# Retention and ELU feed-forward on one core: w_out in 4 KB pieces, features in even and odd tiles, and small moves between engines

## The chip, the cores and the metric

The kernel runs on one core of one Trainium2 chip. Such a core has TensorE (PE) for matmuls, with weight loads shown apart (PEld), VectorE (DVE), ScalarE (ACT) and GpSimd (POOL) for element-wise work, SyncE (SP), which here only issues DMAs, and 16 DMA engines between the chip's memory and SBUF. Matmul results go to PSUM, in banks. The metric is the device time of one execution in microseconds; a time of a kernel is the median of its runs.

## The reference, cut to what matters

```python
# q, k, v: (8, 8, 576, 64), batch x heads x positions x head dim; moe_w_in: (512, 2048); moe_w_out: (2048, 512)
def _attn_ref(q, k, v):
    scores = 1.0 / np.sqrt(64) * np.matmul(q, k.transpose(0, 1, 3, 2))
    gamma = 1.0 - 2.0 ** (-5.0 - np.arange(8))
    rel = pos[:, None] - pos[None, :]
    Dmat = np.where(rel >= 0, gamma[:, None, None] ** rel[None, :, :], 0.0)
    return np.matmul(scores * Dmat[None], v)

def _moe_ref(x, w_in, w_out):              # x: 4608 tokens x 512
    h = x @ w_in
    g = np.where(h > 0.0, h, np.exp(np.minimum(h, 0.0)) - 1.0)
    return g @ w_out
```

The retention result of the eight heads is put side by side into rows of 512, one row for each of 8 x 576 tokens, and goes through the feed-forward layer. All inputs and the output are float32. The hidden features, 2048 of them, are summed over in the second product, so their order does not matter as long as the columns of w_in, g and the rows of w_out agree.

## The kernel before, in words

**Retention.** The decay is split into a factor on q and one on k, so a unit of work is: load q, k and v for one stretch of positions and heads (`load`), multiply q and k by their factors and round to bf16 (`cast`, `cast_qk`, `cast_v`), turn them so that head dimensions lie on partitions (`turn`, a DMA transpose, or `turn_pe`, TensorE transposes into PSUM with a copy back), multiply k by q (`scores`), mask the product within a chunk of 64 (`masks`, on VectorE, tile `pt`), and add what earlier chunks contribute through a running state (`state`, `prefix`, `inter`). The state of a chunk lies in the same PSUM bank (x0 or x1, pool `ps_x`) as the unit's output; VectorE reads it into the tiles `mid` and `end`, and small copies bring them in bf16 into `s_pair` (`put_mid`, `put_end`) or, at the end of a batch, into `s_last` (`put_last`), which the last 64 positions of each batch need much later. `put_x` writes a unit's output, turned, into `xt`. Units are numbered from 0; the first twelve are coarse (256 positions, four heads), so that "the sixth unit" is `load(5)`, `cast(5, ...)` and `turn_pe(5, ...)`. A call `stretch(u)` makes the scores, masks and states of unit u and finishes unit u - 1.

**Feed-forward.** FFN1 (`ffn1`, `ffn1_half`) makes one tile of 128 hidden features for 512 tokens, or two tiles for 256 tokens, with four matmuls per tile over the 512 inputs; the weights that are loaded are 128 columns of `w_in_sb` (tile `ph`). `elu` does the activation with two passes on ScalarE (L607, L610) and one on VectorE (L611), which writes `g`. FFN2 (`ffn2`) multiplies g by `w_out_sb`, 512 wide, over 16 feature tiles into one bank per 128 tokens (tile `pm`), which ScalarE copies out (`ot`).

**Weights.** `weights(k)` lists, for one staging tile of 512 KB, the two DMA sources and the places in SBUF: k = 0 to 7 are w_in, k = 8 to 15 are w_out, with two blocks of 128 features each (L163). `load_w` issues two DMAs of 256 KB on SyncE, each partition receiving 2 KB from one row; `cast_w` rounds each half to bf16, mostly on GpSimd. Staging tiles and q/k tiles share ten buffers.

**The order.** All instructions are pinned in program order on each engine (`pin`), so a wait on one engine holds up all that stands behind it there. Up to the first twelve units the order is written by hand. The first four units come first; then FFN1 of the first 512 tokens, one tile at a time (`one(ft, ...)`), with FFN2 rows behind it: `row(i)` is the two matmuls that add feature tile i to two blocks of output. L834 and L835 say which rows stand behind which tile: 

```python
    behind = {4: (0, 1), 11: ()}
    behind.update({ft: (ft - (3 if ft < 11 else 4),) for ft in range(5, 16) if ft != 11})
```

These tiles' banks come from two pools: even tiles take x0 and x1 in turn, odd tiles the three banks of `ps_h`, of which one holds the second output block. Then the fifth to eighth units are woven with `quad(i)`, four FFN2 matmuls of the other two output blocks, and with halves of FFN1 of the next batch (`some`). From the ninth unit on, lists of FFN1 and FFN2 jobs are mixed by `stage`, and a unit's step is put between them at due times. SyncE issues its loads in the order in which the program names them (L810 to L816, L878, L879, L884), DMA transposes among them.

Of the kernel before, what the change touches and what calls it, by code (L numbers as in the profile page):

```python
# [17 lines left out]
def kernel(  # L18
# [9 lines left out]
    nc = tc.nc  # L28
# [5 lines left out]
    P = 128  # L34
# [4 lines left out]
    KJ = DM // P  # L39
# [23 lines left out]
    pin = tc.keep_in_program_order  # L63
    def mm(*a, **kw):
        pin(nc.tensor.matmul(*a, **kw))  # L65
# [77 lines left out]
    w_in_sb = const.tile([P, KJ, DF], BF16, name="w_in_sb")  # L143
    w_out_sb = const.tile([P, NFT, DM], BF16, name="w_out_sb")
# [3 lines left out]
    tt = {"v": nc.vector.tensor_tensor, "p": nc.gpsimd.tensor_tensor}  # L148
    staged = {}

    def weights(k):
        for h in range(2 * (k < 2)):

            r, c = slice(2 * h * P, 2 * (h + 1) * P), slice(k * 2 * P, (k + 1) * 2 * P)
            yield h, moe_w_in[r, c].rearrange("(j p) c -> p j c", j=2), w_in_sb[:, 2 * h : 2 * h + 2, c]
        for i in (2 * k, 2 * k + 1) if k > 1 else ():
            n, j = divmod(i, KJ)
            if n < KJ:
                c = slice(n * 512, (n + 1) * 512)
                yield i % 2, moe_w_in[j * P : (j + 1) * P, c], w_in_sb[:, j, c]  # L160
            else:
                f = i - KJ * KJ
                yield i % 2, moe_w_out[f * P : (f + 1) * P, :], w_out_sb[:, f, :]  # L163

    def load_w(k):
        staged[k] = raw.tile([P, 2, 4, 2, D], FP32, name="rqk", tag="rqk").rearrange("p i h e d -> p i (h e d)")
        for h, src, dst in weights(k):
            pin(nc.sync.dma_start(staged[k][:, h] if k > 1 else staged[k][:, h].rearrange("p (j c) -> p j c", j=2), src))  # L168

# [11 lines left out]
    def fine(u):  # L181
        return seq[u][0] >= 3
# [7 lines left out]
    def load(u, what="qkv"):  # L190
        b, T, w = seq[u]
        if u not in rawt:
            rawt[u] = (raw.tile([P, 2, 4, 2, D], FP32, name="rqk", tag="rqk"),
                       raw.tile([P, 4, 2, D], FP32, name="rv", tag="rv", bufs=5))
        rqk, rv = rawt[u]
        parts = [{"q": (rqk[:, 0], q), "k": (rqk[:, 1], k), "v": (rv, v)}[x] for x in what]
        if fine(u):
            t = u % 4
            for dst, src in parts:
                pin(nc.sync.dma_start(  # L200
                    dst.rearrange("p a e d -> p (a e) d"), src[b, :, t * P : (t + 1) * P, :].rearrange("h p d -> p h d"),
                ))
            return
        for dst, src in parts:
            pin(nc.sync.dma_start(  # L205
                dst.rearrange("p h e d -> p h (e d)"),
                src[b, 4 * w : 4 * w + 4, 2 * P * T : 2 * P * (T + 1), :].rearrange("h (p e) d -> p h (e d)", e=2),
            ))

    def cast_qk(u, i, eng, es=(0, 1)):  # L210
        b, T, w = seq[u]
        if fine(u):
            pin(tt[eng](  # L213
                natt[u][0][:, i].rearrange("p e h d -> p (e h) d"), rawt[u][0][:, i].rearrange("p a e d -> p (a e) d"),
                (gqf, gkf)[i][:, u % 4].unsqueeze(2).to_broadcast([P, H, D]), ALU.mult,
            ))
            return
        x = rawt[u][0][:, i].rearrange("p h e d -> p e h d")
        g = (gq, gk)[i][:, 2 * T : 2 * T + 2, 4 * w : 4 * w + 4].unsqueeze(3).to_broadcast([P, 2, 4, D])
        for e in es:  # L220
            pin(tt[eng](natt[u][0][:, i, e], x[:, e], g[:, e], ALU.mult))  # L221

    def cast_v(u, eng):
        pin(engines[eng](natt[u][1], rawt[u][1]))  # L224

    def cast(u, q="p", k="p", v="p"):
        if u >= NS:
            return
        qkn = nat.tile([P, 2, 2, 4, D], BF16, name="qkn", tag="qkn")
        vn = nat.tile([P, 4, 2, D], BF16, name="vn", tag="vn", bufs=5)  # L230
        natt[u] = qkn, vn
        if q:
            cast_qk(u, 0, q)
        if k:
            cast_qk(u, 1, k)
        if v:
            cast_v(u, v)

    def flat(u):
        return natt[u][0].rearrange("p i e h d -> p (i e h d)")  # L240

    def turn(u):
        if u < NS:
            trt[u] = tpool.tile([P, 8, P], BF16, name="qkT", tag="qkT")
            pin(nc.sync.dma_start_transpose(trt[u], flat(u)))
# [19 lines left out]
    def new_x():  # L265
        for c in range(2):
            xps[c] = ps_x.tile([P, 512], FP32, name="x", tag=f"x{c}")
        begun.clear()
# [105 lines left out]
    def drop(u):  # L374
        natt.pop(u)
        ptt.pop(u)
        trt.pop(u)
        score_ps.pop(u, None)
# [75 lines left out]
    def blocks(dst, src, eng):  # L454
        for i in range(2):
            pin(engines[eng](dst[half(i), :, half(i)], src[half(i)]))  # L456

    def put_last(b, w, src, eng):
        for i in range(2):
            pin(engines[eng](s_last[b % 3][half(w), :, i], src[half(i)]))  # L460
# [4 lines left out]
    def put_end(u, eng="p"):  # L465
        b, T, w = seq[u]
        if T:
            put_last(b, w, total[w], eng)
        else:
            blocks(s_first[w], total[w], eng)  # L470
# [68 lines left out]
    def stretch(u, put="p", end="p"):  # L539
        old = u - 1 in natt and u - 1 in ptt  # L540
        rider = late.pop() if late else None
        new_x()
        if rider is not None:
            inter_rider(rider)
        if old:
            inter(u - 1)
        if u < NS:
            scores(u)
            if fine(u):
                state(u)  # L550
            masks(u)
        if u in rides:
            scores_rider(rides[u])
        if old:
            values(u - 1)
        if rider is not None:
            values_rider(rider)
        if u < NS and not fine(u):
            state(u)
        if old:  # L560
            put_x(u - 1)
            drop(u - 1)
        if rider is not None:
            put_rider(rider)
        if u < NS:
            if fine(u):
                prefix_fine(u)
            else:
                prefix_mid(u, put)
                prefix_end(u, end)  # L570
        if u in rides:
            masks_rider(rides[u])
            late.append(rides[u])
# [16 lines left out]
    def xt_tile(g):  # L590
        if g == B:
            return xtail
        if g not in xts:
            xts[g] = xpool.tile([P, 2, KJ, 2 * P], BF16, name="xt", tag="xt")
        return xts[g]
# [22 lines left out]
    def ffn1(g, ft, pool=None, tag="ph", **kw):  # L618

        ph = (pool or ps_h).tile([P, TG], FP32, name="ph", tag=tag)  # L620
        for j in range(KJ):
            mm(ph, w_in_sb[:, j, ft * P : (ft + 1) * P], xt_tile(g)[:, :, j], start=(j == 0), stop=(j == KJ - 1))
        gtile(g, ft // 2, 0)
        elu(gts[g, ft // 2][:, :, ft % 2], ph, pairs, **kw)

    def ffn1_half(g, p, hf, **kw):

        ph = ps_h.tile([P, TG], FP32, name="ph", tag="ph")
        for f in range(2):
            for j in range(KJ):  # L630
                mm(ph[:, f * 2 * P : (f + 1) * 2 * P], w_in_sb[:, j, (2 * p + f) * P : (2 * p + f + 1) * P],
                   xt_tile(g)[:, hf, j], start=(j == 0), stop=(j == KJ - 1))
        elu(gtile(g, p, hf).rearrange("p f n -> p (f n)"), ph, **kw)

# [121 lines left out]
    first = [ps_x.tile([P, TG], FP32, name="ph", tag=f"x{ft}") for ft in range(2)]  # L756

    def part(ft, *js):
        for j in js:
            mm(first[ft], w_in_sb[:, j, ft * P : (ft + 1) * P], xt_tile(0)[:, :, j], start=(j == 0), stop=(j == KJ - 1))  # L760

    masks(3, (1,))
    cast_w(0, " v")
# [46 lines left out]
    for kk in (4, 5, 10, 11, 6, 7, 12, 13):  # L810
        load_w(kk)
    load(4)
    for kk in (14, 15):
        load_w(kk)
    for u in range(5, 10):
        load(u)  # L816
    F = {0: {}, 1: dict(pool=ps_h, tag="ph"), 2: dict(pool=ps_h, tag="ph"), 3: {}}

    def row(ft):
# [11 lines left out]
    for kk in (8, 9, 4, 5, 10, 11):  # L831
        cast_w(kk)

    behind = {4: (0, 1), 11: ()}  # L834
    behind.update({ft: (ft - (3 if ft < 11 else 4),) for ft in range(5, 16) if ft != 11})  # L835
    for ft in range(4, 8):
        one(ft, behind[ft])
    for kk in (6, 7, 12, 13):
# [3 lines left out]
    cast(4, "p", "p", None)  # L842
    cast_w(14)
    cast_w(15)
    put_end(2)
    put_end(3)
    half1 = f1h(1, 0)

    def some():
# [7 lines left out]
    quad(0)  # L857
    turn_pe(4, "vs", pool=ps_x, tags=("x0", "x1"))
    cast_v(4, "s")
    cast(5, "v", "p", None)  # L860
    quad(1)
    quad(2)
    stretch(4, "p")
# [5 lines left out]
    cast_v(5, "s")  # L869
    cast(6, "v", "p", None)  # L870
    quad(3)
    stretch(5, end=None)
    quad(4)
    turn_pe(6, "vs")
    cast_v(6, "s")
    cast(7, "v", "p", None)
    put_end(5)
    turn(7)  # L878
    load(10)  # L879
    quad(5)  # L880
    stretch(6, "p")
# [76 lines left out]
    c = [j for g, hf in twos[E:] for j in f2(g, (2 * hf, 2 * hf + 1))]  # L958
    at = {id(x): i // 8 for i, x in enumerate(a)}
    jobs = weave(a, c)  # L960
    n = 0
    phases = [[] for _ in range(len(ones) - E + 1)]
    for x in jobs:
        n = at.get(id(x), n)
# [50 lines left out]
```

## Time and profile before

| What | us |
|---|---|
| Median of 3 runs | 303.43 (303.04 to 304.12) |
| The profiled execution | 303.18 |
| its span, first to last instruction | 301.4 |
| TensorE busy | 289.8 (96%) |
| ScalarE busy | 210.8 (70%) |
| GpSimd busy | 175.4 (58%) |
| VectorE busy | 175.1 (58%) |
| DMA, mean over the span | 180 GB/s |

In rows of the profile a line such as `L611 DVE SCALAR_TENSOR_TENSOR g<-e,ph` is line, engine, operation, and output from inputs by the program's names. In a timeline a row has start, duration, engine, line, what, how many instructions, and in brackets the idle time of the engine before it with what ended it; a row with x4 stands for four neighbouring instructions. In the chain of work a row has start, duration and what the chain went through. [...] Some matmul records are missing, so a row may say x3 for four matmuls. SPq rows are the issuing of DMAs on SyncE.

### The profile page before, as it was taken

To read this page: it belongs to the slowest core of one execution; us is meant where nothing else is said; L and a number is where in the kernel's file an instruction comes from. 1 tells how busy PE (TensorE), PEld (TensorE's weight loads), DVE (VectorE), ACT (ScalarE), POOL (GpSimd) and SP (SyncE) were. 2 spreads that over 40 slices of the span, in tenths; PEclk is the share of its full clock that TensorE was granted. 3 is DMA by queue.
4 is the path that set the end of the run, shared out by engine and by line. 5 is a ranking of instruction groups with operands and counts; after the bars stand their busy time and mean duration, and the time that the engine had idled before them with its cause. 6 is when DMAs were issued, how large, how long until landed. Compare 5 with 4: busy or idle time off the path is not lost.

```text
span 301.4 us, 9038 instructions
## 1 busy us (share of the span) xinstructions
PE 289.8 (96%) x3587; PEld 176.0 (58%) x3624; DVE 175.1 (58%) x355; ACT 210.8 (70%) x430; POOL 175.4 (58%) x344
## 2 busy tenths in 40 slices
PE   8789999999999999999999999999999999999995
PEld 5444446776676666667767675544444444456654
DVE  4846557765556756666776766768675734332210
ACT  4669847967766777767777887777777776764531
POOL 5689887687957585858496887468852300011000
PEclk9999999999999999999999999999999999999999
DMA  7999999989999999999999999999860100001012
GB/s 208 307 360 353 353 306 285 220 244 165 248 191 214 176 221 211 199 201 207 202 188 213 195 202 211 190 237 177 173 90 37 38 35 36 37 35 70 37 70 70
DMA packets 133418, 54.33 MB, mean 180 GB/s; under 512 B 107712, under 2 KB 127424, under 8 KB 133376
## 3 DMA queue, kind: packets, MB, share of 16 engines
q1 hardware_dynamic: 130624, 45.04, 77.3%
q0 software_dynamic: 2672, 8.65, 8.5%
q8 instruction: 28, 0.46, 0.7%
q14 instruction: 14, 0.11, 0.1%
q10 hardware_dynamic: 80, 0.07, 0.1%
HBM read 36.70 MB, written 9.44 MB: 153 GB/s over the span
## 4 chain that ended last, share of the span: by engine, by line
PE 80%; DMA 10%; SPq 3%; issue 2%; ACT 2%; DVE 1%; POOL 0%; DVEq 0%
PE pm L65 36%; PE ph L65 36%; DMA rqk<-in_moe_w_out_dram 5%; PE x L65 4%; SPq L205 3%; PE sc L65 3%; DMA rqk<-in_q_dram 2%; DMA rqk<-in_moe_w_in_dram 2%; PE pe L65 1%; ACT ph L610 1%; DVE pt L318 1%; ACT e L607 1%; SPq L168 1%; PE ptr L256 0%; DVE qkn L221 0%
## 5 line engine op out<-in xcount | busy, mean ns | idle before, releaser
L611 DVE SCALAR_TENSOR_TENSOR g<-e,ph 128x512 bf16<-128x512 f32 x128 | 86.4, 686 | 84.6 <-ACT ph L610 81.1
L65 PE MATMUL ph<-xt,w_in_sb 128*128 128x256 bf16 (+1 forms) x768 | 128.7, 308 | 0.2 <-DVE g L611 0.2
L65 PE MATMUL pm<-w_out_sb,g 128*128 128x512 bf16 x478 | 123.8, 379 | 3.1 <-issue 2.1
L607 ACT ACTIVATE e<-ph 128x512 f32<-128x512 f32 x144 | 86.0, 597 | 52.5 <-PE ph L65 51.8
L65 PEld LDWEIGHTS <-w_in_sb 128*128 128x128 bf16 x896 | 86.4, 98 | 50.3 <-issue 0.6
L610 ACT ACTIVATE ph<-ph 128x512 f32<-128x512 f32 x144 | 83.9, 591 | 0.0
L65 PEld LDWEIGHTS <-g 128*128 128x128 bf16 x512 | 48.7, 98 | 43.8
L664 POOL DMA_DIRECT2D out_dram<-ot x35 | 19.9, 569 | 44.6 <-ACT ot L654 44.2
L436 POOL CAST s_fine<-run 64x256 bf16<-64x256 f32 x40 | 15.8, 396 | 42.2 <-DVE run L405 33.2
L654 ACT COPY ot<-pm 128x512 f32<-128x512 f32 x35 | 20.4, 587 | 15.1 <-PE pm L65 15.0
L611 DVE SCALAR_TENSOR_TENSOR gt<-e,ph 128x512 bf16<-128x512 f32 x16 | 10.9, 687 | 18.8 <-ACT ph L610 17.2
L213 POOL TENSOR_TENSOR qkn<-rqk,gqf 128x512 bf16<-128x512 f32 x20 | 21.1, 1053 | 0.4
L213 POOL TENSOR_TENSOR qkn<-rqk,gkf 128x512 bf16<-128x512 f32 x20 | 20.9, 1046 | 0.0
L221 POOL TENSOR_TENSOR qkn<-rqk,gk 128x256 bf16<-128x256 f32 x23 | 14.2, 638 | 4.4 <-DMA rqk<-in_k_dram 4.2
L65 PE MATMUL ph<-xtail,w_in_sb 128*128 128x256 bf16 x128 | 16.5, 273 | 0.0
L368 ACT CAST xt<-x 128x256 bf16<-128x256 f32 x40 | 12.9, 378 | 4.8 <-PE x L65 4.8
L405 DVE TENSOR_TENSOR run<-sc,run 128x256 f32<-128x256 f32 x35 | 14.9, 424 | 1.2
L224 POOL CAST vn<-rv 128x512 bf16<-128x512 f32 x24 | 14.6, 608 | 1.4
L318 DVE TENSOR_TENSOR pt<-sc,mask 128x1024 bf16<-128x1024 f32 x11 | 13.4, 1218 | 0.5 <-PE sc L65 0.4
L311 DVE TENSOR_TENSOR pt<-sc,mask_t 128x512 bf16<-128x512 f32 x20 | 13.7, 684 | 0.0
L456 POOL CAST s_pair<-mid 64x128 bf16<-64x128 f32 x24 | 6.9, 288 | 10.7 <-DVE mid L405 6.4
L442 POOL CAST s_fine<-run 64x256 bf16<-64x256 f32 x30 | 11.8, 395 | 1.8
(94 smaller groups left out, 261.4 us busy)
## 6 DMA issues: line engine op xcount, KB each, us to landing
rqk<-in_q_dram SPq DMA_DIRECT2D x32, 256.0 KB, 4.4
rqk<-in_k_dram SPq DMA_DIRECT2D x32, 256.0 KB, 5.2
rv<-in_v_dram SPq DMA_DIRECT2D x32, 256.0 KB, 5.6
out_dram<-ot POOLq DMA_DIRECT2D x31, 256.0 KB, 3.5
rqk<-in_moe_w_in_dram SPq DMA_DIRECT2D x16, 256.0 KB, 5.9
rqk<-in_moe_w_out_dram SPq DMA_DIRECT2D x16, 256.0 KB, 5.4
rqt<-in_q_dram SPq DMA_DIRECT2D x8, 128.0 KB, 5.5
rqt<-in_k_dram SPq DMA_DIRECT2D x8, 128.0 KB, 4.9
```

Of the source, the lines that this page charges most:

```text
L65: pin(nc.tensor.matmul(*a, **kw))
L213: pin(tt[eng](natt[u][0][:, i].rearrange("p e h d -> p (e h) d"), rawt[u][0][:, i].rearrange("p a e d -> p (a e) d"), (gqf, gkf)[i][:, u % ...
L221: pin(tt[eng](natt[u][0][:, i, e], x[:, e], g[:, e], ALU.mult))
L224: pin(engines[eng](natt[u][1], rawt[u][1]))
L318: pin(nc.vector.tensor_tensor(ptt[u].rearrange("p i h n -> p (i h) n"), sc.rearrange("p i (h n) -> p (i h) n", h=2), m.to_broadcast([P, 4, ...
L405: pin(nc.vector.tensor_tensor(dst, a, b, ALU.add))
L436: pin(nc.gpsimd.tensor_copy(s_fine[u % 2][half(1), :, i], new[half(i), 0]))
L607: pin(nc.scalar.activation(e, ph, AF.Exp))
L610: pin(nc.scalar.activation(ph, ph, AF.Relu))
L611: pin(nc.vector.scalar_tensor_tensor(dst, view(e), -1.0, view(ph), ALU.add, ALU.min))
L654: pin(nc.scalar.copy(ot, pm))
L664: pin((queue or nc.gpsimd).dma_start(dst, src))
```

## The change

- A new function `features(ft)` names the 128 features of a tile: of each 256 neighbouring features the even ones for an even tile, the odd ones for an odd tile. FFN1 takes its weights from these columns of `w_in_sb`, that is with a step of two (`ffn1`, `ffn1_half`, `part`).
- w_out follows: a partition now holds two neighbouring rows. For k = 9 to 15 both come in one DMA of 512 KB, 4 KB for each partition; k = 8 is still loaded by two DMAs, of every second row.
- FFN2 rows of the first 512 tokens stand four tiles behind FFN1 throughout; before, it was three for tiles 5 to 10, with two rows behind tile 4 and none behind tile 11.
- The last states of the third and fourth unit are copied by ScalarE instead of GpSimd and stand later in the program, behind `cast_v(4, "s")`.
- q of the sixth unit is scaled by GpSimd instead of VectorE.
- The tenth unit's loads stand behind the eighth unit's turn on SyncE instead of ahead of it.
- `stretch(5, "p", ...)` and `put_end(5, "p")` name the value that was the default.

```diff
+    def features(ft):
+        return slice(ft // 2 * 2 * P + ft % 2, (ft // 2 + 1) * 2 * P, 2)
+
     def weights(k):
...
                 f = i - KJ * KJ
-                yield i % 2, moe_w_out[f * P : (f + 1) * P, :], w_out_sb[:, f, :]
+                yield i % 2, moe_w_out[features(f), :], w_out_sb[:, f, :]
...
     def load_w(k):
         staged[k] = raw.tile([P, 2, 4, 2, D], FP32, name="rqk", tag="rqk").rearrange("p i h e d -> p i (h e d)")
+        if k > KJ * KJ // 2:
+            n = k - KJ * KJ // 2
+            pin(nc.sync.dma_start(
+                staged[k].rearrange("p e c -> p (e c)"),
+                moe_w_out[2 * n * P : 2 * (n + 1) * P, :].rearrange("(p e) c -> p (e c)", e=2),
+            ))
+            return
...
-            mm(ph, w_in_sb[:, j, ft * P : (ft + 1) * P], xt_tile(g)[:, :, j], start=(j == 0), stop=(j == KJ - 1))
+            mm(ph, w_in_sb[:, j, features(ft)], xt_tile(g)[:, :, j], start=(j == 0), stop=(j == KJ - 1))
...
-                mm(ph[:, f * 2 * P : (f + 1) * 2 * P], w_in_sb[:, j, (2 * p + f) * P : (2 * p + f + 1) * P],
+                mm(ph[:, f * 2 * P : (f + 1) * 2 * P], w_in_sb[:, j, features(2 * p + f)],
...
-            mm(first[ft], w_in_sb[:, j, ft * P : (ft + 1) * P], xt_tile(0)[:, :, j], start=(j == 0), stop=(j == KJ - 1))
+            mm(first[ft], w_in_sb[:, j, features(ft)], xt_tile(0)[:, :, j], start=(j == 0), stop=(j == KJ - 1))
...
-    for kk in (14, 15):
-        load_w(kk)
-    for u in range(5, 10):
-        load(u)
+    load_w(14)
+    load_w(15)
+    load(5)
+    load(6)
+    load(7)
+    load(8)
...
-    behind = {4: (0, 1), 11: ()}
-    behind.update({ft: (ft - (3 if ft < 11 else 4),) for ft in range(5, 16) if ft != 11})
+    behind = {ft: (ft - 4,) for ft in range(4, 16)}
...
     cast_w(14)
     cast_w(15)
-    put_end(2)
-    put_end(3)
     half1 = f1h(1, 0)
...
     cast_v(4, "s")
-    cast(5, "v", "p", None)
+    put_end(2, "s")
+    put_end(3, "s")
+    cast(5, "p", "p", None)
...
-    stretch(5, end=None)
+    stretch(5, "p", end=None)
...
-    put_end(5)
+    put_end(5, "p")
     turn(7)
+    load(9)
     load(10)
```

## The prediction

> **What bounds the kernel now.** I read the page first, then the busy time by stretch, the list of TensorE's waits, the chain of work over the early part, and last the engines' timelines around the waits found. The page:
>
> ```profile
> span 301.4 us, 9038 instructions
> ...
> PE 289.8 (96%) x3587; PEld 176.0 (58%) x3624; DVE 175.1 (58%) x355; ACT 210.8 (70%) x430; POOL 175.4 (58%) x344
> ```
>
> TensorE is busy for 96% of the span. The busy time by stretch (stretch, its length, then each engine) tells where the rest lies:
>
> ```profile
> 18.70:37.90 19.20, 19.08 (x102) 8.67 (x97) 10.11 (x16) 16.54 (x33) 17.66 (x30) 1.00 1.04 351
> 37.90:50.70 12.80, 11.80 (x193) 6.98 (x195) 9.47 (x18) 7.53 (x17) 10.18 (x23) 1.00 1.14 299
> 50.70:62.00 11.30, 10.84 (x149) 8.79 (x149) 7.00 (x13) 10.50 (x23) 8.10 (x19) 1.00 1.18 252
> ```
>
> and so do the waits of TensorE from 18.5 us to the end:
>
> ```profile
> PE ptr L256 <- DVE end L405: 0.6, 1, 0.6
> ...
> PE ph L65 <- DVE g L611: 0.2, 1, 0.2
> ```
>
> So there is little to win: 1.0 us of idle time from 37.9 to 50.7, 0.5 us up to 62. The early waits are single ones, and after 62 us TensorE has none on another engine, so what is saved or lost before is carried to the end. The first 18.7 us do not contain what the diff moves. The chain shows where the 0.6 us comes from:
>
> ```profile
> 29.17 5.51 DMA rqk<-in_moe_w_out_dram
> ...
> 34.74 7.05 DMA rqk<-in_q_dram
> 41.80 0.02 issue
> 41.82 0.30 DVE qkn L221
> ```
>
> It is the DMA stream, weights and then the sixth unit's q, landed at 41.79. VectorE scales that q first and only then masks the fifth unit and reads its states, which sit in the bank into which the sixth unit is turned.
>
> **The change part by part.**
>
> *FFN2 rows one tile later (L834, L835).* TensorE, then VectorE, around 24 us, and from the whole chain the pace of eight 256-wide and four 512-wide matmuls:
>
> ```profile
> 23.50 1.03 PE L65 MATMUL pm<-w_out_sb,g 128*128 128x512 bf16 x3
> 24.54 1.02 PE L65 MATMUL ph<-xt,w_in_sb 128*128 128x512 bf16 x4
> ```
> ```profile
> 23.80 0.69 DVE L611 SCALAR_TENSOR_TENSOR g<-e,ph 128x512 bf16<-128x512 f32 x1 [0.31 <-ACT ph L610]
> ```
> ```profile
> 82.75 0.87 PE ph L65 x8
> ...
> 261.44 0.86 PE pm L65 x4
> ```
>
> A 512-wide matmul takes 0.216 us, a 256-wide one 0.109. Rows 0 and 1 (four matmuls, one not recorded) fill 23.50 to 24.36; tile 5 starts at 24.54, 0.05 us after the g that ends at 24.49. That is tile 2's, whose bank tile 5 takes: a hidden wait of 0.18 us. With row 1 moved behind tile 5, TensorE arrives at 23.93 and still waits until 24.54. The displaced row (2 x 0.216 us) is paid at tile 11, which had no row behind it. Cost +0.43 us on the path; it takes away no wait that the list shows.
>
> *The sixth unit's q on GpSimd, last states on ScalarE (L845, L846, L860).* TensorE, VectorE, ScalarE and GpSimd around 42 us:
>
> ```profile
> 39.22 0.61 PE L256 MATMUL ptr<-ident,qkn 128*128 128x128 bf16 x8
> 39.66 1.89 PE L65 MATMUL pm<-w_out_sb,g 128*128 128x512 bf16 x8
> 41.48 0.42 PE L65 MATMUL sc<-qkT 64*64 64x128 bf16 x16
> 41.73 0.29 PE L65 MATMUL x<-vn,qkn 64*64 64x64 bf16 x16
> 41.96 1.90 PE L65 MATMUL pm<-w_out_sb,g 128*128 128x512 bf16 x7
> 44.49 0.61 PE L256 MATMUL ptr<-ident,qkn 128*128 128x128 bf16 x8 [0.63 <-DVE end L405]
> ```
> ```profile
> 41.82 0.85 DVE L221 TENSOR_TENSOR qkn<-rqk,gq 128x256 bf16<-128x256 f32 x2 [1.56 <-DMA rqk<-in_q_dram]
> 42.60 1.21 DVE L318 TENSOR_TENSOR pt<-sc,mask 128x1024 bf16<-128x1024 f32 x1
> 43.73 0.28 DVE L416 COPY mid<-x 128x128 f32<-128x128 f32 x1
> 44.14 0.29 DVE L405 TENSOR_TENSOR end<-x,mid 128x128 f32<-128x128 f32 x1
> ```
> ```profile
> 43.68 1.07 ACT L654 COPY ot<-pm 128x512 f32<-128x512 f32 x2 [2.71 <-PE pm L65]
> 45.13 0.58 ACT L257 COPY qkT<-ptr 128x512 bf16<-128x512 bf16 x1 [0.38 <-PE ptr L256]
> ```
> ```profile
> 40.23 1.34 POOL L173 CAST w_out_sb<-rqk 128x512 bf16<-128x512 f32 x2 [0.89 <-DMA rqk<-in_moe_w_out_dram]
> 41.51 1.66 POOL L460 CAST s_last<-end 64x128 bf16<-64x128 f32 x4
> 43.24 1.18 POOL L221 TENSOR_TENSOR qkn<-rqk,gk 128x256 bf16<-128x256 f32 x2
> ```
>
> Before, the eight matmuls from 41.96 end at 43.69 and the transposes start at 44.49: a wait of 0.80 us. After, TensorE is 0.43 later: scores from 41.91 to 42.33. VectorE, free of q, starts pt when they end, about 42.38; mid comes 1.13 later (43.73 - 42.60), end 0.41 after mid (44.14 - 43.73) and lasts 0.29: done at 44.21, transposes at 44.27 (0.06 later, as now). TensorE arrives at 44.12, so a wait of 0.15 remains: -0.65 us.
>
> What covers the moves: GpSimd gives up 1.66 us of states and takes q for 1.18 us, the price of its k. The four small copies on ScalarE have no row there; GpSimd's 1.66 us for them is the nearest, zero and twice that the ends. ScalarE idles for 2.71 us before its ot copies, so even 2.7 us would be covered and I take 0; without that cover the ot copies would start up to 0.6 us later. Late next is ScalarE's copy of the turned k. It stands behind the ot copies, which move 0.43 later (44.11 to 45.18), and would end at 45.7, about when TensorE wants the scores of the sixth unit: +0.03.
>
> *w_out in 4 KB pieces (L163, L167, L168).* SyncE's issues: weights in 2 KB pieces, then units in 512 B pieces, then the eighth unit's turn:
>
> ```profile
> 21.96 2.27 SPq L168 DMA_DIRECT2D rqk<-in_moe_w_out_dram  x4
> 24.55 2.27 SPq L168 DMA_DIRECT2D rqk<-in_moe_w_in_dram  x4
> ...
> 41.77 0.78 SPq L205 DMA_DIRECT2D rqk<-in_q_dram  x1
> ...
> 44.40 0.73 SPq L205 DMA_DIRECT2D rqk<-in_q_dram  x1
> ...
> 50.43 1.97 SPq L245 DMA_TRANSPOSE qkT<-qkn  x1
> ```
>
> Four weight transfers of 256 KB pass in 2.6 us (0.65 each), three unit transfers in 2.63 (0.88 each). At 8 and 32 pieces on each of 16 engines that is 81 and 27 ns a piece, of which some 9 ns do not grow with its size. 512 KB in 4 KB pieces would save 8 x 9 ns, 0.07 us; the seven of them 0.5 us, with zero as one end and 7 x 8 x 27 ns = 1.5 us as the other. The path gains none of it: TensorE waits for no weights, and the q that was waited for now stands on GpSimd behind the last w_out. Against it, 512 KB land as one, so the first of two casts starts up to 0.65 us later. For the last piece: landed about 40.9 (41.57 less one cast of 0.67), less 0.5; two casts of 1.34 end at 41.7, q at 42.9, k at 44.1. The k half is turned from 44.49 on (four of eight transposes behind 44.27), so this is covered: 0. If the stream gains nothing, k ends at 44.6: +0.1.
>
> *The eighth unit's turn ahead of the tenth unit's loads (L816, L878).* SyncE had issued those loads by 50.43, so the issue gains next to nothing, and the transfer at most the three loads ahead of it, 3 x 0.88 = 2.6 us. No wait of TensorE is on a turned unit, so 0. The loads, and the ninth unit's turn behind them, go back by as much; two units' work lies between them and their use, so 0 again, and at most 2.6 if nothing lay between.
>
> *Tiles of even and odd features (L622, L631, L760).* No instruction is added, but the 896 weight loads of FFN1 read every second column:
>
> ```profile
> L65 PE MATMUL ph<-xt,w_in_sb 128*128 128x256 bf16 x512 | 65.4, 273 | 0.2 <-DVE g L611 0.2
> ...
> L65 PE MATMUL ph<-xtail,w_in_sb 128*128 128x256 bf16 x128 | 16.5, 273 | 0.0
> ```
> ```profile
> L65 PEld LDWEIGHTS <-w_in_sb 128*128 128x128 bf16 x896 | 86.4, 98 | 50.3 <-issue 0.6 <-DVE xt L372 0.2
> ```
>
> No row has a strided load. Eight pairs of a load and a 128-wide matmul took 0.44 us (39.22 to 39.66), so a contiguous load repeats within 55 ns. If the stride halves its speed it needs 110 ns, at the edge of the 109 ns of the 256-wide matmul that covers it. Lower end 0 (a gain has no room: the matmuls set the pace), upper end the 98 ns doubled with nothing overlapped, 640 x 87 ns = 56 us. I take 0, by the pairs, which are nearest.
>
> [...]
>
> **Sum.** +0.43 - 0.65 + 0.03 = -0.2 us. The profiled execution took 303.18 (span 301.4, 1.8 around it), so 303.0 on its scale. The median of the runs shown, 303.43, is 0.25 above it, so 303.2 as a median.
>
> **Rivals.**
> - *Strided loads are paid (slower).* For it: nothing shows them free, and half speed is already at the edge. [...] It decides from 109 ns a load: at 112, 640 x 3 ns = 1.9 us, 305.1; at the far end 359. [...]
> - *The row's move is free (faster).* If tile 5 does not hang on tile 2's bank, -0.65 + 0.03 stands alone: 302.8. Against it: the 0.05 us between that g and tile 5.
> - *GpSimd becomes the bound.* It is busy 17.66 of 19.20 us up to 37.9. If the whole landings put its casts back by 0.4 us more than reckoned, the transposes wait for k instead of VectorE; at a further 0.65 us the second term of the sum is gone, 303.9.
> - *The move of q does nothing,* if in other executions q lands early enough and the 0.80 us are not there: +0.43 alone, 303.9.
>
> **How the numbers follow.** Forecast 0.5, strided loads 0.2 (0.17 near 305, 0.03 far out), the other three 0.1 each. Runs of this kernel can tell about 0.3%, 0.9 us, from no change. Strided loads lie beyond it; of the others, with a spread of runs from 303.04 to 304.12, some tenth falls out on either side: faster 0.12, same 0.61, slower 0.27. Range 302.5 (row free, a low run) to 305.0 (loads at 112 ns); the likeliest's own is 302.7 to 303.9.
>
> **What would show it.** Right: tile 5 still at 24.5 with 0.6 us idle ahead of it; pt of the fifth unit right behind its scores; a wait of 0.2 us or less before the sixth unit's transposes; eight 256-wide matmuls still in 0.87 us. Wrong: eights above 0.87, a wait for GpSimd before transposes or rows, tile 5 before 24.5.

## The result, and the profile after

The changed kernel takes 304.70 us in the median of 21 runs (303.14 to 306.86), the kernel before 303.37 beside it (302.23 to 304.63, 21 runs): a ratio of 1.0047, 95% interval 1.0030 to 1.0065. Forecast were 303.2 and a change of -0.2; it is slower by 1.3 us. Below, turns and loads are named as in the code: `turn(8)` is the ninth unit's turn, `load(9)` the tenth unit's loads.

The profiled execution took 305.54 (span 303.8). From the page, and TensorE's waits from 18.5 us on (who waited for whom: total, times, longest):

```profile
span 303.8 us, 9068 instructions
...
PE 293.6 (97%) x3624; PEld 175.6 (58%) x3624; DVE 175.5 (58%) x353; ACT 212.1 (70%) x434; POOL 174.7 (58%) x342
```
```profile
PE sc L65 <- DMA qkT<-qkn: 1.4, 2, 1.0
...
PE ph L65 <- DVE g L622: 0.4, 1, 0.4
```

TensorE's 3.8 us more of busy time than before are mostly a matter of records: of the same 3624 matmuls, 37 were not recorded before. The busy time by stretch, as before but 0.81 us later, since this execution starts its FFN1 by that much later:

```profile
19.51:38.71 19.20, 18.75 (x102) 8.50 (x95) 10.64 (x17) 16.21 (x33) 16.55 (x30) 1.00 1.02 360
38.71:51.51 12.80, 12.80 (x199) 7.31 (x198) 8.94 (x17) 9.05 (x21) 10.40 (x21) 1.00 1.00 263
51.51:62.81 11.30, 10.89 (x150) 8.78 (x148) 6.83 (x13) 10.49 (x23) 8.12 (x19) 1.00 0.94 234
62.81:80.00 17.19, 15.83 (x225) 10.75 (x223) 10.46 (x17) 10.67 (x22) 12.75 (x27) 1.00 1.26 226
```

The 1.0 us of idle time in the second stretch is gone (0.3 of it were gaps in which a matmul was not recorded, which leaves 0.6 to 0.8 of waiting), the first lacks some 0.3 more, and after 62.8, where TensorE had no wait on another engine, 1.4 us are idle. The wait of the sixth unit's transposes for VectorE is gone from the list, the wait of tile 5 for g is longer, and a new one is the largest: scores wait for a DMA transpose. TensorE's timeline, before and after:

```profile
18.72 0.60 PE L65 MATMUL ph<-xt,w_in_sb 128*128 128x512 bf16 x2
...
64.65 0.42 PE L65 MATMUL sc<-qkT 64*64 64x128 bf16 x16
...
69.68 0.42 PE L65 MATMUL sc<-qkT 64*64 64x128 bf16 x16
```
```profile
19.53 0.61 PE L65 MATMUL ph<-xt,w_in_sb 128*128 128x512 bf16 x2
...
25.35 1.02 PE L65 MATMUL ph<-xt,w_in_sb 128*128 128x512 bf16 x4 [0.45 <-DVE g L622]
...
43.20 1.90 PE L65 MATMUL pm<-w_out_sb,g 128*128 128x512 bf16 x8
45.09 0.61 PE L267 MATMUL ptr<-ident,qkn 128*128 128x128 bf16 x8
...
66.49 0.42 PE L65 MATMUL sc<-qkT 64*64 64x128 bf16 x16 [1.03 <-DMA qkT<-qkn]
...
71.92 0.42 PE L65 MATMUL sc<-qkT 64*64 64x128 bf16 x16 [0.33 <-DMA qkT<-qkn]
```

TensorE's rows overlap (the eight transposes from 45.09 last 0.61 us, and the next matmuls start 0.44 after them, at 45.53), so gaps given "by the starts" leave the overlap out.

FFN1 of the first tokens starts 0.81 us later (19.53 against 18.72). In the traces of this document it starts between 18.67 and 19.98 us, with and without the parts of the change. Here the delay is already there when SyncE issues the first weights (10.62 us against 9.79), ahead of anything the diff moves. Counted from that start, the first half tile of the next batch begins 0.1 us earlier than before (51.39 - 19.53 against 50.66 - 18.72), and the scores that use `turn(8)` begin 1.0 us later (46.96 against 45.93); those that use `turn(9)` 1.4 later (52.39 against 50.96). 0.8 of start, -0.1, and 1.5 of turns with what follows them (an idle stretch of 1.20 by the starts, and the 0.33 of the last row) make up most of the 2.4 us between the spans.

SyncE's issues, after and (one row) before, then GpSimd's row for k of `turn(7)`, after, and the busy time from 50 to 52 us, before and after (last two columns: mean share of the 16 DMA engines, GB/s):

```profile
46.51 0.82 SPq L216 DMA_DIRECT2D rv<-in_v_dram  x1
50.80 1.34 SPq L256 DMA_TRANSPOSE qkT<-qkn  x1
52.19 0.57 SPq L216 DMA_DIRECT2D rqk<-in_q_dram  x1
...
55.50 0.38 SPq L216 DMA_DIRECT2D rv<-in_v_dram  x1
56.00 4.29 SPq L256 DMA_TRANSPOSE qkT<-qkn  x1
...
63.50 5.14 SPq L256 DMA_TRANSPOSE qkT<-qkn  x2
```
```profile
54.86 1.25 SPq L245 DMA_TRANSPOSE qkT<-qkn  x1
```
```profile
49.28 1.50 POOL L232 TENSOR_TENSOR qkn<-rqk,gk 128x256 bf16<-128x256 f32 x2
```
```profile
50.00:52.00 2.00, 1.99 (x16) 1.50 (x16) 1.36 (x3) 1.39 (x4) 1.50 (x6) 1.00 1.10 287
```
```profile
50.00:52.00 2.00, 2.00 (x58) 1.43 (x51) 1.90 (x4) 1.28 (x4) 1.53 (x5) 1.00 0.15 36
```

`turn(7)` cannot be issued before GpSimd has scaled its k (49.28 + 1.50 = 50.78; issued 50.80). In the kernel before, three loads of `load(9)` were under way then. Now they stand behind the waiting turn, SyncE issues nothing from 47.33 to 50.80, and the queue runs empty: 36 GB/s instead of 287. Then `load(9)`, `load(10)`, `turn(8)` and three output stores of GpSimd want to pass together; the issue of `turn(8)` alone took 4.29 us (1.25 before). The chain of work of the changed kernel goes through `turn(9)`:

```profile
63.41 0.09 POOL vn L235
63.50 8.38 DMA qkT<-qkn
71.88 0.04 issue
```

Counted from the start of FFN1, `turn(9)` is issued when it was before (63.50 - 19.53 and 62.69 - 18.72 are both 43.97), but lands 3.7 us later. By this chain, taking away the wait for `turn(8)` alone would not help: TensorE would wait longer for `turn(9)`.

### The profile page after: what moved, and what is told of

Read it like the earlier page. It is cut to its first block, busy times and chain, and to the rows that moved or that the text cites. A ratio compares the mean times of both kernels' runs of the same rounds, so it can differ in the third digit from the quotient of the medians.

```text
span 303.8 us, 9068 instructions
## 1 busy us (share of the span) xinstructions
PE 293.6 (97%) x3624; PEld 175.6 (58%) x3624; DVE 175.5 (58%) x353; ACT 212.1 (70%) x434; POOL 174.7 (58%) x342
## 4 chain that ended last, share of the span: by engine, by line
PE 85%; DMA 4%; ACT 3%; SPq 3%; POOL 2%; issue 1%; DVE 1%; POOLq 0%
PE pm L65 39%; PE ph L65 37%; PE x L65 4%; PE sc L65 3%; DMA qkT<-qkn 3%; SPq L216 3%; DMA rqk<-in_k_dram 2%; ACT ph L621 1%; PE pe L65 1%; ACT e L618 1%; POOL qkn L232 1%; POOL s_pair L467 1%; PE ptr L267 0%; DVE pt L329 0%; DVE g L622 0%
## 5 line engine op out<-in xcount | busy, mean ns | idle before, releaser
L65 PE MATMUL pm<-w_out_sb,g 128*128 128x512 bf16 x512 | 129.8, 379 | 0.0
L447 POOL CAST s_fine<-run 64x256 bf16<-64x256 f32 x40 | 16.0, 400 | 41.9 <-DVE run L416 34.0
L65 PE MATMUL sc<-qkT 64*64 64x64 bf16 (+1 forms) x512 | 11.6, 204 | 1.6 <-DMA qkT<-qkn 1.4
```

The costliest lines, as they stand in the source:

```text
L447: pin(nc.gpsimd.tensor_copy(s_fine[u % 2][half(1), :, i], new[half(i), 0]))
```

## The experiments

Each kernel ran beside the kernel before on the same chip; a ratio is to that, with a 95% interval. The chip of the result is not recorded and is called the first here; e1 to e4 ran on a second (which may be the same), e5, e6, e7 and e11 on a third, e12, e15 and the second runs of e2 and of the changed kernel on a fourth, e16, the third run of the changed kernel and the second ones of e1 and e11 on a fifth. From e7 on the expectations count loads as the code does ("the ninth unit's loads" are `load(9)`), turns as above.

**e1: the loads back.**

```diff
     load(8)
+    load(9)
...
     turn(7)
-    load(9)
     load(10)
```

> The changed kernel with the tenth unit's loads ahead of the eighth unit's turn again; all else of the change stays. Theory (the moved loads make the turns of the ninth and tenth unit late): TensorE's waits on turned units, 1.4 us in the changed kernel, vanish; time 1.5 us below the changed kernel, near 303.2, 0.2 below the kernel before. Rival (the 4 KB pieces or the other moves disturb the DMA stream, and the turns are late for that): the waits stay at 1 us or more and the time stays near 304.7. In both, tile 5 still waits 0.6 us and the sixth unit's transposes 0.15.

Measured: 303.43 (303.10 to 303.88), ratio 0.9981 (0.9961 to 1.0001). No wait for a turned unit. The timeline and the stretch from 50 to 52 us:

```profile
64.78 0.42 PE L65 MATMUL sc<-qkT 64*64 64x128 bf16 x16
...
69.82 0.42 PE L65 MATMUL sc<-qkT 64*64 64x128 bf16 x16
```
```profile
50.00:52.00 2.00, 1.86 (x15) 1.41 (x17) 1.40 (x3) 1.37 (x4) 1.43 (x6) 1.00 1.11 286
```

All the rest of the change is in this kernel; only the position of three loads differs. Counted from the start of FFN1 the two scores begin 0.1 us sooner than before, but to the end of the span both take 282.7 us: one trace shows no gain from the rest of the change.

**e2: that part alone.** The kernel before, with `load(9)` behind `turn(7)`.

```diff
-    for u in range(5, 10):
+    for u in range(5, 9):
...
     turn(7)
+    load(9)
     load(10)
```

> The kernel before with one edit: the tenth unit's loads behind the eighth unit's turn. Theory (late turns): TensorE waits for the turned ninth and tenth units, 1 to 2 us together, none elsewhere that is new; time 1 to 2 us above the kernel before, 304.4 to 305.4. Rival (disturbance by the 4 KB pieces): no such wait, time within 0.3 of the kernel before.

Measured: 304.75 (303.31 to 306.02), ratio 1.0034 (1.0014 to 1.0054). So the part alone costs about 1 us in the median. Its trace (an execution of 304.19) doesn't show the wait: `turn(8)` landed at 64.69, 1.0 us ahead of the scores at 65.68, where the kernel before has 3.2. What this trace has over that of the kernel before, 1.0 us, lies ahead of the moved loads in the main: FFN1 starts 0.38 later, and the sixth unit's transposes wait 0.5 longer. Once more, on the fourth chip:

> The kernel before with only the ninth unit's loads behind the eighth unit's turn, once more, for a second trace: the first took 304.2 us and showed no wait on a turned unit, but only 1.0 us between the landing of the ninth unit's turn and its use, where before has 3.2. Theory: what is lost in the median of 1.1 us is lost in such executions in which that 1.0 us is used up, so either the wait shows now, or the slack is again below 1.5 us and the time near before.

Measured: 303.88 (302.64 to 306.14), 1.0012 (0.9988 to 1.0036); the trace is that of an execution of 303.17, and `turn(8)` landed at 64.23, 0.4 us ahead of its use. The second interval includes a ratio of 1, and the wait was never seen in this kernel; that it makes the executions above 304.5 is inferred from the spent slack.

**e3 and e4: the other moves alone.** e3 is the kernel before with q of the sixth unit on GpSimd and the last states on ScalarE; e4 the kernel before with rows four tiles behind.

```diff
-    put_end(2)
-    put_end(3)
...
-    cast(5, "v", "p", None)
+    put_end(2, "s")
+    put_end(3, "s")
+    cast(5, "p", "p", None)
```
```diff
-    behind = {4: (0, 1), 11: ()}
-    behind.update({ft: (ft - (3 if ft < 11 else 4),) for ft in range(5, 16) if ft != 11})
+    behind = {ft: (ft - 4,) for ft in range(4, 16)}
```

> The kernel before with q of the sixth unit on GpSimd and the last states on ScalarE, nothing else. By the sum of the prediction: the wait of 0.80 us before the sixth unit's transposes falls to about 0.15, time 0.65 us below the kernel before (302.8). Rival (q lands early enough in other executions): no wait there to remove, time the same.

> The kernel before with the FFN2 rows four tiles behind throughout, nothing else. By the sum of the prediction: tile 5 starts 0.6 instead of 0.18 us after TensorE is free, 0.43 us more up to there. Whether it reaches the end: VectorE's mask of the fifth unit waits for q, not for TensorE, so a part is hidden in the 0.80 us wait before the sixth unit's transposes, which then shrinks by up to 0.43; time 0 to 0.43 us above the kernel before. Rival (the row is free): tile 5 starts earlier than 0.6 us after, and nothing changes.

Measured: e3 303.76, ratio 1.0002 (0.9983 to 1.0020); e4 303.93, 1.0002 (0.9984 to 1.0021). TensorE's timeline of e3, then its waits in e4:

```profile
30.20 0.59 PE L65 MATMUL pm<-w_out_sb,g 128*128 128x512 bf16 x2 [0.78 <-POOL w_out_sb L173]
...
44.16 1.90 PE L65 MATMUL pm<-w_out_sb,g 128*128 128x512 bf16 x7
46.06 0.73 PE L256 MATMUL ptr<-ident,qkn 128*128 128x128 bf16 x8
```
```profile
PE ph L65 <- DVE g L611: 0.7, 1, 0.7
PE ptr L256 <- DVE end L405: 0.4, 1, 0.4
```

In e3 the transposes follow with a gap of 0.16 by the starts, as reckoned, but this execution started late (FFN1 at 19.98), and rows three tiles behind then wait 0.78 for w_out. In e4 tile 5 waits 0.6 to 0.7, as reckoned, and the transposes' wait is 0.52 by the starts instead of 0.80: part of the 0.43 comes back there. Neither effect is large enough for the medians.

**e5 and e6: the even and odd tiles, without and with the 4 KB pieces.** The kernel before with `features` in FFN1 and in the rows of w_out; e6 also with the DMA of 512 KB.

```diff
-                yield i % 2, moe_w_out[f * P : (f + 1) * P, :], w_out_sb[:, f, :]
+                yield i % 2, moe_w_out[features(f), :], w_out_sb[:, f, :]
...
-            mm(ph, w_in_sb[:, j, ft * P : (ft + 1) * P], xt_tile(g)[:, :, j], start=(j == 0), stop=(j == KJ - 1))
+            mm(ph, w_in_sb[:, j, features(ft)], xt_tile(g)[:, :, j], start=(j == 0), stop=(j == KJ - 1))
```

> The kernel before with nothing but the tiles of even and odd features: the 896 weight loads of FFN1 read every second column, w_out is still loaded in 2 KB pieces (its rows chosen to match), and the order of the work is untouched. If strided loads cost nothing, as the pace of the changed kernel says: a weight load of 98 ns in the mean, eight 256-wide matmuls still in 0.87 us, time within 0.3% of before. If they are paid and something else in the changed kernel hid it: loads above 109 ns and 1.9 us or more on top of before.

> The kernel before with the tiles of even and odd features and w_out in 4 KB pieces, rows, engines and the order of the loads as before. Prediction's cost of the pieces: 0, the stream at most 0.5 us shorter and hidden. But rows stay three tiles behind, and 512 KB land as one, so the first row of a pair can come later: if rows wait for it, a wait of TensorE for the cast w_out of up to 0.7 us shows in the early part and the time rises by as much; if not, time within 0.3% of before.

Measured: e5 304.16, ratio 1.0009 (0.9984 to 1.0033); e6 303.79, 1.0003 (0.9982 to 1.0024). The strided loads in e5 by groups (busy, mean ns), its chain, then q of the sixth unit and TensorE's transposes in e6:

```profile
L65 PEld LDWEIGHTS <-w_in_sb 128*128 128x128 bf16 x896 | 86.7, 98 | 51.0 <-issue 1.4 <-POOL w_in_sb L176 0.4
```
```profile
70.41 0.87 PE ph L65 x8
```
```profile
40.87 1.03 DVE L231 TENSOR_TENSOR qkn<-rqk,gq 128x256 bf16<-128x256 f32 x2
```
```profile
44.36 0.61 PE L266 MATMUL ptr<-ident,qkn 128*128 128x128 bf16 x8
```

A strided load takes the same 98 ns, eight matmuls the same 0.87 us. (In e5's profiled execution, 306.49, the granted clock was 0.95 from 18.70 to 50 us.) In e6 VectorE has q at 40.87 instead of 41.82, though FFN1 started 0.4 later, and the gap ahead of the transposes is 0.16 by the starts: in this trace the pieces alone take away the wait for which the change also moved q, though the median shows no gain. No row waits for a w_out that lands as one.

**e7: `turn(8)` ahead of `load(10)`.**

```diff
     turn(7)
     load(9)
-    load(10)
...
     turn(8)
+    load(10)
     load(11)
```

> The changed kernel with the ninth unit's turn ahead of the tenth unit's loads instead of behind them; the ninth unit's loads still stand behind the eighth unit's turn. Theory: the waits for turned units come from what stands ahead of those turns on SyncE's queue after the queue has run empty around 51 us. The empty stretch (50 to 52 us near 36 GB/s) stays, the ninth unit's turn has three loads of 0.88 us less ahead of it, so its wait of 1.2 us goes or falls below 0.3; the tenth unit's loads land later and with them its turn, whose wait of 0.33 stays or grows to at most 1.5. Time between 303.4 and 304.7. Rival, that the extra time of the changed kernel has nothing to do with when a turn lands: ninth unit's wait may go, the time stays at 304.7.

Measured: 303.50 (303.21 to 304.06), 0.9985 (0.9966 to 1.0003). The queue runs empty all the same, but the turn is quick:

```profile
50.00:52.00 2.00, 1.84 (x20) 1.42 (x16) 1.45 (x3) 1.32 (x4) 1.43 (x6) 1.00 0.22 46
```
```profile
54.96 1.25 SPq L256 DMA_TRANSPOSE qkT<-qkn  x1
```

It landed at 60.55, 4.3 us ahead of its use; no wait. `turn(9)` landed 0.4 ahead of its use (69.48, 69.87), so the wait that was expected to stay or grow is gone too. So the empty stretch by itself costs nothing, and the loss hangs on when `turn(8)` passes.

**e15: two units between the turns, no empty stretch.** e1 with `turn(8)` behind `load(11)`.

```diff
-    turn(8)
     load(11)
+    turn(8)
```

> The changed kernel with the ninth unit's loads back ahead of the eighth unit's turn, and the ninth unit's turn now behind the eleventh unit's loads: again two units' loads between the two turns, as in the changed kernel (there the ninth's and the tenth's), but nothing missing ahead of the eighth unit's turn, so the queue does not run empty around 51 us. If it is the two units between the turns that makes the ninth unit's turn land late (they put back its issue, which took 4.29 us in the changed kernel), it lands near 66 again and TensorE waits for it as there, up to 1.5 us: 304.0 to 305.0. If the empty stretch is needed for it, the turn lands three loads of 0.88 us later than with one unit between, about 63.5 instead of 60.6 to 61.5, ahead of its use at 64.8: no wait, within 0.2 us of the kernel with only the loads put back, 303.4.

Measured: 303.68 (303.16 to 305.28), 0.9993 (0.9969 to 1.0018). The trace is the longest execution of the twelve, late from its start (FFN1 at 19.84), with 1.1 us of waits for w_out and none for a turn: `turn(8)` landed at 65.85, as late as the first theory said, and still 0.7 ahead of its use, which had moved back with all else. Neither expectation fits whole: two units between the turns make it late, but not late enough.

**What the packets say.** Each turn moves 1024 packets of 256 B. Read from the trace's packets and landings for `turn(8)` (us; "took" is from first to last packet):

| Kernel | first packet | took | landed | used | TensorE waited |
|---|---|---|---|---|---|
| before | 57.35 | 2.9 | 61.46 | 64.65 | no |
| changed | 60.10 | 5.1 | about 66.4 | 66.49 | 1.03 |
| changed, second trace | 59.28 | 5.95 | about 66.0 | 66.02 | 0.80 |
| changed, third trace | 59.59 | 5.3 | 65.71 | 65.75 | 0.60 |
| e1, loads back | 56.52 | 2.9 | not recorded | 64.78 | no |
| e2, e2b, turn only | 60.84, 60.31 | 3.2, 3.3 | 64.69, 64.23 | 65.68, 64.61 | no |
| e3, engines only | 59.68 | 1.4 | 64.21 | 66.35 | no |
| e7, turn(8) ahead of load(10) | 56.35 | 3.0 | 60.55 | 64.83 | no |
| e15, two units between | 62.45 | 2.9 | 65.85 | 66.59 | no |
| e12, below | 60.01 | 5.6 | 66.40 | 66.45 | 0.37 |

In e4, e5, e6 and e11 it took 2.9 and no scores waited. Where TensorE waits, the transfer starts late and also takes about twice as long (5.1 to 5.95 us against 2.9). In the changed kernel's first trace, counted from the start of FFN1, the first packet is 1.9 us later than before and the transfer 2.1 longer.

The longer transfer has more passing beside it. Between its first and last packet 272 KB of output stores pass before; in the three traces of the changed kernel 560 to 620 KB of stores and 140 to 170 KB of loads do. With the turn's own 256 KB that makes 170 to 200 KB per us in all four, so the turn is stretched by what shares its time. That pace is no constant: in e2 it is 240. Packets of over a us are no mark of it: there are 22 before and 4 to 8 in the changed kernel, where more packets take some 160 or 330 ns instead of 18.

**The changed kernel again, and the loads back again.** The changed kernel on the fourth chip; then both side by side on the fifth.

> The changed kernel as it is, once more, for a second trace. Theory: the waits for the ninth and tenth units' turns show again, 0.5 to 2 us together, and the empty stretch of the queue around 51 us. Rival: they are an accident of the one execution, and none shows.

> The changed kernel as it is, now on one chip beside the same kernel with the loads put back. Theory: it is 0.3 to 1.3 us slower than that one in the median, and where its profiled execution is slow (above 304.5 us) it shows TensorE waiting for turned units and a transfer of the ninth unit's turn of 5 us or more. Rival: no difference between the two beyond 0.2 us.

> The changed kernel with only the ninth unit's loads put back ahead of the eighth unit's turn, beside the changed kernel itself. Theory: 303.4 as at first, 0.3 to 1.3 us below the changed kernel, no wait for a turned unit.

Measured: 303.73 (303.26 to 306.40), 1.0013 (0.9992 to 1.0034) on the fourth chip; on the fifth 304.16 (303.04 to 305.80), 1.0018 (0.9996 to 1.0040), and with the loads back 303.60 (303.07 to 304.37), 0.9987 (0.9972 to 1.0002). The wait is in every trace of the changed kernel; the second and the third:

```profile
66.02 0.42 PE L65 MATMUL sc<-qkT 64*64 64x128 bf16 x16 [0.80 <-DMA qkT<-qkn]
...
71.54 0.42 PE L65 MATMUL sc<-qkT 64*64 64x128 bf16 x16 [0.41 <-DMA qkT<-qkn]
```
```profile
65.75 0.42 PE L65 MATMUL sc<-qkT 64*64 64x128 bf16 x16 [0.60 <-DMA qkT<-qkn]
```

The loss varies by chip: 1.3, 0.2 and 0.4 us in the medians against before, the last two with intervals that include a ratio of 1. On the fifth chip alone the intervals of the changed kernel and of e1 overlap; what tells them apart is the wait in the traces, and over all chips the long executions. Of the changed kernel's 45 executions 21 took over 304.5 us, of the kernel before 12 of the 91 beside them, with the loads back none of 24.

**e16: the stores held.** The changed kernel, with GpSimd's three output stores held until `cast(10)`; loads and turns untouched.

```diff
     def some():
         half1.pop(0)()
         settle()
-        tick()
+        if not held:
+            tick()
+
+    held = [True]
...
     turn(10)
+    held.clear()
     while half1:
```

> The changed kernel with GpSimd's three output stores (128 x 512 each), which it issues around 55.5 us, held until the tenth unit is scaled, some 10 us later; the loads and turns stand as in the changed kernel. If those stores lengthen the transfer of the ninth unit's turn, it takes 3 us or less even in a slow execution, lands by 63.5, TensorE waits for no turned unit, and the time is near the kernel with the loads put back, 303.4. If they do not, the transfer still takes 5 us or more in a slow execution, or the time stays with the changed kernel's.

Measured: 303.72 (303.13 to 304.49), 0.9992 (0.9978 to 1.0006), on the chip where the changed kernel took 304.16 (the intervals overlap). Stores on GpSimd, and the scores:

```profile
65.83 2.33 POOL L675 DMA_DIRECT2D out_dram<-ot  x4
```
```profile
65.03 0.42 PE L65 MATMUL sc<-qkT 64*64 64x128 bf16 x16
...
70.07 0.42 PE L65 MATMUL sc<-qkT 64*64 64x128 bf16 x16
```

With the stores away, `turn(8)` passes from 58.41 to 61.33, 2.9 us, and lands at 62.02, 3.0 ahead of its use; no wait. The stores are thus part of the loss: they put its first packet back by about 1 us and lengthen it by 2 to 3. Before, they overlap the turn too (57.1 to 61.6 against 57.4 to 60.3), but two thirds of them pass after its last packet or ahead of its first; in the changed kernel the turn comes 1.0 to 1.5 us behind the first store packet and most of them pass beside it. Why the order comes out so stays open.

**e11 and e12: a version below both kernels.** e11 is e1 with rows 0 and 1 at tile 4 again and none at tile 5; e12 the same rows and engine moves on the kernel before, with contiguous weights, 2 KB pieces and `load(9)` where it was.

```diff
     behind = {ft: (ft - 4,) for ft in range(4, 16)}
+    behind.update({4: (0, 1), 5: ()})
```

> The changed kernel with the ninth unit's loads back ahead of the eighth unit's turn, and with the FFN2 rows as before up to tile 4 and from tile 6 three or four behind chosen so that no tile of the early FFN1 is left without a row that the kernel before gave it: tile 4 carries rows 0 and 1, tile 5 none, tile 6 and later the row four behind. Theory: two rows at tile 4 fill the stretch in which tile 5 waits for its bank, so the 0.43 us that the later rows cost is not paid, and the 0.65 us that q on GpSimd and the last states on ScalarE save stays: some 0.4 us below the kernel with only the loads put back, 303.0 on the scale where before is 303.4, a ratio near 0.998. Rival, that the saving of q is used up elsewhere: within 0.1 us of before.

> The changed kernel with the ninth unit's loads put back and the mixed rows, once more: rows 0 and 1 at tile 4, none at tile 5, from tile 6 on the row four behind. Theory: 0.43 us below the kernel with only the loads put back, 303.0 to 303.3, a ratio near 0.998 to before.

> The kernel before with the sixth unit's q on GpSimd, the last states on ScalarE and the mixed rows (rows 0 and 1 at tile 4, none at tile 5, from tile 6 on the row four behind), but contiguous weight loads and w_out in 2 KB pieces, and the loads where they were before. If the 4 KB pieces do nothing for the path, this is as fast as the same kernel with them, 0.4 to 0.6 us below before. If they matter, by letting w_out land sooner, this one is slower than that, with a wait of TensorE for a row of w_out or for the sixth unit's q: within 0.3% of before.

Measured: e11 303.33 (302.76 to 304.49), 0.9980 (0.9960 to 0.9999), and 303.16 (302.73 to 304.00), 0.9985 (0.9970 to 0.9999); e12 303.32 (302.26 to 305.38), 0.9991 (0.9971 to 1.0011). TensorE in e11, tile 5 and the rows ahead of it, without a marked wait (0.19 by the starts, where before has 0.18):

```profile
23.66 1.03 PE L65 MATMUL pm<-w_out_sb,g 128*128 128x512 bf16 x3
24.71 1.67 PE L65 MATMUL ph<-xt,w_in_sb 128*128 128x512 bf16 x7
```

Beside e1 on the fifth chip its median is 0.44 us lower (303.16 against 303.60), near the 0.43 of the late row, though the intervals overlap. It has the lowest ratios here, 0.15 to 0.20% below the kernel before, with both intervals just under 1. e12's trace is its longest execution (305.38): w_out, q and the turns are all late in it, and the scores wait for turns though `load(9)` stands ahead:

```profile
66.45 0.42 PE L65 MATMUL sc<-qkT 64*64 64x128 bf16 x16 [0.37 <-DMA qkT<-qkn]
```

So a late stream can spend the turn's slack without the change too. Whether the 4 KB pieces protect against it, as that trace suggests, the intervals of e11 and e12 don't tell.

## Why the prediction was wrong

- **Rows one tile later, +0.43: right.** Tile 5 starts 5.82 us after the first FFN1 matmul in both kernels (25.35 - 19.53, 24.54 - 18.72), after 0.61 idle by the starts instead of 0.18; e4 shows the wait alone, and e11 without it has a median 0.44 below e1's, though their intervals overlap.
- **q on GpSimd, states on ScalarE, -0.65: right.** The gap ahead of the transposes fell from 0.80 to 0.16, and with the late row they start 0.21 us sooner after FFN1's start than before (25.56 against 25.77), as the sum had it. The four states took 1.22 us on ScalarE, within the bounds of zero and 3.3, and were covered. That in other executions the wait isn't there to be won was a rival's reason; e6 shows one such case, where w_out in 4 KB brings q sooner.
- **ScalarE's late copies, +0.03: too low.** From the sixth unit's transposes to the seventh's TensorE takes 3.21 us (45.09 to 48.30) instead of 3.08 (44.49 to 47.57). Most of this stands ahead of the matmuls that read v (47.18): its cast, on ScalarE behind the copies, ends at 47.13. So 0.1 of the 0.2 forecast is lost again.
- **4 KB pieces, 0: right for the path; for the stream 0.5 or more.** Taken were 0.5 us, with 1.5 as the upper end. Counted from the start of FFN1, q of the sixth unit lands at 23.08 us before and 22.59 after, the 0.5 that was taken, but at 21.73 in e6, 1.35 sooner. Other traces have it at 22.9 to 24.1 with 2 KB pieces and at 21.6 to 23.5 with 4 KB, so no single pair gives the size.
- **Strided weight loads, 0: right.** At a step of 2 a load takes 98 ns, as with neighbouring columns before, and eight 256-wide matmuls take 0.87 us in both. The 1.9 us and more of the rival did not show.
- **The eighth unit's turn ahead of the tenth unit's loads, 0: wrong, and nearly the whole miss.** The step said that no wait of TensorE is on a turned unit, that two units' work lies between the later turn and its use, and "at most 2.6 if nothing lay between". What lay between was not two units' work but 3.2 us for `turn(8)` and 2.3 for `turn(9)` (landings 61.46 and 67.41 before, used at 64.65 and 69.68). Neither was worked out. And the delay was more than 2.6: `turn(8)` landed 4.9 us later, of which 0.8 is the late start of that execution; the 4.1 left exceed the 3.2. For `turn(9)` 3.7 exceed the 2.3. Three things were left out. `turn(7)` waits at the head of SyncE's queue until 50.8 for GpSimd, so loads behind it do not merely change places: the queue empties (36 GB/s against 287). What was not moved then passes later, with the next unit's loads and the stores; and `turn(8)` itself, beside those, takes 5 to 6 us instead of 2.9. Putting the loads back (e1), the turn sooner (e7) or the stores away (e16) each removes the wait.
- **Price.** 1.5 us in the profiled execution; against the forecast of -0.2 the median of the first 21 runs is 1.5 higher. On the fourth and fifth chip the excess over -0.2 is 0.4 and 0.6. The range up to 305.0 held 304.70, but for strided loads, not for this. Among the rivals none was a transfer that lands late.

256 KB of unit loads pass in 0.88 us here (three in 2.63, before). The 256 KB of a turn, from first to last packet, took 1.45 us at 52 us of the changed kernel, where the queue had run empty, and at best 0.97 (`turn(9)` in e2), close to that. Beside stores and loads `turn(8)` took 2.9 to 5.95 in all traces but e3's (1.4).

## What to carry to other kernels

A transfer without a wait in the profile still has a slack, its landing against its first use; before anything is moved ahead of or behind it in a queue, work out that slack and compare it with the delay. Behind a DMA that waits for an engine SyncE issued nothing here (47.33 to 50.80 us), so what is put there is delayed by the wait as well as by its place. A transposing DMA deserves a margin of several us where stores run beside it (5.1 to 5.95 us with 560 to 620 KB of stores beside it, 2.9 with 272 KB); here a gain of 0.65 us on TensorE was lost to waits of 1.03 and 0.33 us for two of them.

## What the runs showed of the hardware

- Loading every second bf16 column as TensorE weights cost nothing beside 256-wide matmuls: 98 ns a load, 109 ns a matmul (eight in 0.87 us), as with neighbouring columns.
- A DMA transpose of 256 KB took between 0.97 (`turn(9)` in e2) and 5.95 us from first to last of the same 1024 packets; holding the stores brought it from 5.3 (third trace) to 2.9 on the same chip.
- The issue of a transfer can itself be long: the row of `turn(8)` on SyncE is 4.29 us instead of 1.25, and the loads behind it on SyncE stand for as long. A long issue and a long transfer need not go together: in e12 the row is 1.66, and the transfer takes 5.6.
- The start of the work differs by about 1 us between traces (first FFN1 matmul at 18.67 to 19.98 us), and late ones spend slack elsewhere: 0.78 us for a row of w_out in e3.
